# A one-core attention and MLP kernel: batch 0's Q by head halves, its first weights in row chunks, a tightened head chain, and batch 1's K^T V one step later

## The chip, the cores and the metric

The kernel runs on one core of one Trainium2 chip. The metric is the device time in microseconds (us) of one execution, as the median of several executions. Beside the time, each execution reports the **span**: the length from the core's first to its last instruction on the profile's clock. The time is a little longer than the span. I call the difference the **tail**. Each execution also reports the mean clock that the tensor engine was granted, 1.0 being full speed. Engines are called as the profile calls them: PE is the tensor engine's multiplies, PEld its weight loads, DVE the vector engine, ACT the scalar engine, POOL the GpSimd engine.

## The reference

```python
# q, k, v: (8 batches, 8 heads, 576 rows, 64), fp32
kv  = einsum('bhsd,bhse->bhde', k, v)            # 64 x 64 for each head
out = einsum('bhsd,bhde->bhse', q, kv)
rms = sqrt(mean(out * out, axis=-1) + 1e-6)
x   = (out / rms * g_norm)  # heads side by side: 4608 rows x 512
h   = x @ w_in              # 512 x 2048
g   = where(h > 0, h, exp(min(h, 0)) - 1)
return g @ w_out            # 2048 x 512
```

The kernel goes through nine groups of 512 rows: the first 512 of each of the eight batches, then the eight remainders of 64. Only the first group (batch 0) and the start of the second (batch 1) concern us. "Chunk c" is one of the four blocks of 128 columns of x, two heads each. "Half u" is two chunks.

## The kernel before

Loads are issued in this order: Q of batch 0, then K and V by chunk, then w_in by columns.

```python
    fetch_q(0)
    ...
    for c in range(4):
        fetch_packed_kv("k", 0, slice(c, c + 1))
        ...
        fetch_packed_kv("v", 0, slice(c, c + 1))
    edges = (0, 512, 768, 1280, 1664, 2048)
    for lo, hi in zip(edges, edges[1:]):
        load_w_in(slice(lo, hi))
    load_w_out(0, 4)
    fetch_packed_q(1)
    ...
```

The head of the kernel works on batch 0 chunk by chunk. Each chunk takes K^T V with its cast, the "scores" `se` (K^T V applied to Q), a square, a mean over 64 rows by a matmul, a logarithm, an exponential (together the reciprocal root), and a scale into `x0`. Idle matmuls on zeros stand between; they compute nothing and are meant to keep the tensor engine busy. Then come 24 products of x with the first 768 columns of w_in.

```python
    # ... chunks 0 to 2 alike, idle(...) between
    exp_first(1)
    idle(idle_ps, 1)
    kv_first(3)
    scale_first(0)
    idle(idle_ps, 1)
    mean0[2] = bank(2)
    mean_first(2)
    log_first(2)
    se0[3] = bank(3)
    se_first(3)
    square_first(3)
    exp_first(2)
    idle(bank(0), 2)
    scale_first(1)
    scale_first(2)
    # ... first(fs, cs): products of column blocks fs with chunks cs
    first((0, 1, 2, 3), (0,))
    mean0[3] = bank(2)
    mean_first(3)
    log_first(3); exp_first(3); scale_first(3)      # (one line each in the kernel)
    first((0, 1, 2, 3), (1, 2))
    first((4,), (0, 1, 2))
    first((0, 1, 2, 3), (3,))
    first((5,), (0, 1, 2))
    first((4, 5), (3,))
```

Batch 1's attention is woven into batch 0's second matrix product, `mm2` (output matmuls):

```python
    for j in range(J):                  # J = 4
        mm2_quarter(0, j, 1)
        if j == 1:
            at["kvu0"]()                # K^T V of half 0
        if j == 2:
            at["seu0"](scores)          # its scores, squares, sums
            at["sq0"]()
            at["sum0"]()
    for j in range(J):
        mm2(0, j, 8, 10)
        if j == 1:
            at["kvu1"]()
            at["inv0"]()
            at["mulu0"]()               # the two scales of half 0, on DVE
    ...
    for j in range(J):
        mm2(0, j, 10, 12)
        if j == 1:
            at["inv1"]()
            at["xu0"](scores[:, 0, :])  # eight transposes of half 0
```

## Time and profile before

| | before |
|---|---|
| time, median (range) | 284.17 us (284.08 to 284.18) |
| the execution with the profile | 284.47 us, span 282.7 |
| head ends (first of the next 24 matmuls, L465) | 20.43 us |
| batch 1's MLP starts | 46.85 us |
| PE busy | 98% of the span |

PE is busy nearly all the time, so a gain must come from removing work or from starting useful work sooner. The lines themselves are in the prediction.

### The profile page before, as it was taken

Reading aid. Unit: us, or ns where it says so; the run is one execution under the profiler, and the core shown is the slowest. Engines: PE = TensorE matmul, PEld = TensorE weight load, DVE = VectorE, ACT = ScalarE, POOL = GpSimd, SP = SyncE. Lnnn points to the kernel's source line nnn. Section 1 sums busy time; section 2 is a strip of 40 time slices with the busy share of each in tenths; the row PEclk is TensorE's granted clock in tenths of the full one; section 3 lists DMA queues with packets and bytes.
Section 4 is the critical chain, followed back from the end, with each engine's and each line's share of the span. In section 5 each row is a group of like instructions: output and inputs, shape, how many; then the busy total and the mean of one; then the engine's idle time right before and its main releaser. Section 6 shows DMA issues by size and latency. Waiting matters only on the chain.

```text
span 282.7 us, 5187 instructions
## 1 busy us (share of the span) xinstructions
PE 277.2 (98%) x2146; PEld 129.7 (46%) x2146; DVE 159.3 (56%) x231; ACT 154.5 (55%) x222; POOL 54.7 (19%) x96
## 2 busy tenths in 40 slices
PE   7999999999999999999999999999999999999994
PEld 3444454445444444444444444444444444444443
DVE  2359443878388646944694468445854585444400
ACT  2779546667487438533863377237923792333311
POOL 7834422261421331005200421012000000000000
PEclk9999999999999999999999999999999999999999
DMA  7999999797993696358935794455233122010122
GB/s 194 203 204 202 208 200 185 220 152 129 187 190 62 154 166 148 74 148 124 196 75 145 93 216 84 116 115 150 55 97 73 78 53 95 0 77 0 74 74 77
DMA packets 56523, 35.99 MB, mean 127 GB/s; under 512 B 32820, under 2 KB 54068, under 8 KB 56500
## 3 DMA queue, kind: packets, MB, share of 16 engines
q0 software_dynamic: 20752, 17.30, 39.9%
q1 hardware_dynamic: 35348, 17.83, 23.7%
q10 hardware_dynamic: 400, 0.52, 0.6%
q8 instruction: 17, 0.28, 0.4%
q14 instruction: 6, 0.05, 0.0%
HBM read 36.70 MB, written 9.44 MB: 163 GB/s over the span
## 4 chain that ended last, share of the span: by engine, by line
PE 95%; DMA 2%; DVE 1%; SPq 0%; issue 0%; ACT 0%
PE h_ps L465 41%; PE o_ps L512 39%; PE o_ps L917 5%; DMA st_q<-in_q_dram 2%; PE at L174 2%; PE bank L674 1%; PE at L465 1%; PE at L201 1%; PE h_ps L674 1%; PE bank L596 1%; PE bank L644 1%; PE se_ps L201 1%; PE kv_ps L174 0%; PE at L185 0%; PE se_ps L413 0%; PE bank L656 0%
## 5 line engine op out<-in xcount | busy, mean ns | idle before, releaser
L465 PE MATMUL h_ps<-xT,w_in_sb 128*128 128x512 bf16 x536 | 125.7, 379 | 0.0
L512 PE MATMUL o_ps<-w_out_sb,gT 128*128 128x512 bf16 x512 | 120.5, 379 | 0.0
L477 ACT ACTIVATE elu_e<-h_ps 128x1024 bf16<-128x1024 f32 (+1 forms) x71 | 70.0, 995 | 79.9 <-PE h_ps L465 78.3
L465 PEld LDWEIGHTS <-w_in_sb 128*128 128x128 bf16 x552 | 52.5, 98 | 63.2 <-DVE xT L333 1.7
L512 PEld LDWEIGHTS <-gT 128*128 128x128 bf16 x512 | 49.4, 98 | 58.4
L488 DVE TENSOR_SCALAR elu_e<-elu_e 128x1024 bf16<-128x1024 bf16 (+1 forms) x75 | 32.3, 431 | 72.9 <-ACT elu_e L477 72.9
L496 DVE TENSOR_TENSOR gT<-elu_e,h_ps 128x1024 bf16<-128x1024 bf16 (+1 forms) x51 | 60.1, 1179 | 5.7 <-DVE elu_e L488 0.5
L525 ACT COPY o_sb<-o_ps 128x512 f32<-128x512 f32 x32 | 18.6, 586 | 15.6 <-PE o_ps L512 15.6
L218 DVE TENSOR_REDUCE ss<-sq 128x16 f32<-128x1024 bf16 x16 | 19.4, 1219 | 10.8 <-ACT sq L213 10.1
L483 ACT ACTIVATE elu_h<-h_ps 128x1024 bf16<-128x1024 f32 (+1 forms) x20 | 19.5, 990 | 0.0
L150 POOL COPY q_bf<-q_pk 128x512 bf16<-128x512 bf16 x24 | 14.6, 638 | 21.6 <-DMA q_pk<-in_q_dram 21.6
L496 DVE TENSOR_TENSOR gT<-elu_e,elu_h 128x1024 bf16<-128x1024 bf16 x20 | 13.8, 692 | 2.9 <-ACT elu_h L483 1.5
L917 PE MATMUL o_ps<-w_out_sb,gT 128*128 128x512 bf16 (+1 forms) x80 | 14.1, 337 | 0.0
L125 POOL COPY gate<-qT 1x1 bf16<-1x1 bf16 x6 | 1.1, 182 | 63.7 <-DMA qT<-q_bf 63.7
L104 POOL DMA_DIRECT2D q_pk<-in_q_dram x14 | 10.6, 762 | 2.8 <-issue 1.1
L229 DVE TENSOR_TENSOR xs<-at,ss 128x512 bf16<-128x512 f32 x16 | 10.3, 682 | 1.2 <-ACT ss L225 1.2
L917 PEld LDWEIGHTS <-gT 128*128 128x128 bf16 x80 | 7.7, 98 | 6.4 <-DVE gT L496 0.4
L213 ACT ACTIVATE sq<-at 128x1024 bf16<-128x1024 f32 x9 | 9.4, 1043 | 1.6 <-PE at L201 1.0
L118 POOL DMA_DIRECT2D k_pk<-in_k_dram x12 | 8.3, 691 | 4.5 <-DMA w_in_sb<-in_moe_w_in_dram 2.9
L596 PE MATMUL bank<-zeros 128*128 128x512 bf16 x20 | 7.8, 515 | 1.2 <-DVE zeros L573 1.2
L118 POOL DMA_DIRECT2D v_pk<-in_v_dram x12 | 8.2, 684 | 3.7 <-DMA w_out_sb<-in_moe_w_out_dram 1.8
L925 ACT COPY o_last<-o_ps 128x512 f32<-128x512 f32 (+1 forms) x5 | 2.5, 501 | 10.8 <-PE o_ps L917 10.8
(79 smaller groups left out, 139.4 us busy)
## 6 DMA issues: line engine op xcount, KB each, us to landing
out_dram<-o_sb SPq DMA_DIRECT2D x16, 512.0 KB, 3.0
q_pk<-in_q_dram POOLq DMA_DIRECT2D x14, 256.0 KB, 4.8
k_pk<-in_k_dram POOLq DMA_DIRECT2D x6, 576.0 KB, 8.3
v_pk<-in_v_dram POOLq DMA_DIRECT2D x6, 576.0 KB, 10.8
st_q<-in_q_dram SPq DMA_DIRECT2D x2, 512.0 KB, 5.1
w_in_sb<-in_moe_w_in_dram POOLq DMA_DIRECT2D x2, 512.0 KB, 8.8
w_out_sb<-in_moe_w_out_dram POOLq DMA_DIRECT2D x2, 512.0 KB, 15.2
w_out_sb<-in_moe_w_out_dram POOLq DMA_DIRECT2D x4, 256.0 KB, 11.8
```

What stands on the lines that cost most here:

```text
L118: nc.gpsimd.dma_start(out=raw[name, b].rearrange("p h j d -> p h (j d)")[:, hs], in_=in_[:, hs])
L150: eng.tensor_copy(out=out_, in_=in_)
L218: nc.vector.reduce_sum(out=ss, in_=sq.rearrange("p c (h e) -> p (c h) e", h=H), axis=AX.X)
L465: nc.tensor.matmul(h_ps[a][:, cs], lhsT=w_in_sb[:, c, f * P : f * P + P], rhs=x(c, cs), start=(c == 0), stop=(c == KC - 1),)
L477: nc.scalar.activation(e[:, lo:hi, :], ps, AF.Exp)
L483: nc.scalar.activation(h[:, lo:hi, :], ps, AF.Relu)
L488: nc.vector.tensor_scalar(out=e[:, lo:hi, :], in0=e[:, lo:hi, :], scalar1=1.0, scalar2=1.0, op0=ALU.min, op1=ALU.subtract,)
L496: nc.vector.tensor_tensor(out=gT[T][:, 2 * i + lo : 2 * i + hi, :], in0=e[:, lo:hi, :], in1=h, op=ALU.add if relu else ALU.max,)
L512: nc.tensor.matmul(o_ps[T, j], lhsT=gT[T][:, f, j * P : j * P + P], rhs=w_out_sb[:, f, :], start=(f == 0), stop=(f == FC - 1),)
L525: nc.scalar.copy(o_sb[T][:, j % 2, :], o_ps.pop((T, j)))
L596: nc.tensor.matmul(ps, lhsT=zeros[:, 0:P], rhs=zeros, start=True, stop=True)
L917: nc.tensor.matmul(ps, lhsT=gT[B][:, f, j * P : j * P + P], rhs=w_out_sb[:, f, cols], start=(f == 0), stop=(f == FC - 1),)
```

## The change

The intent is to start the useful stream sooner. Q of batch 0 comes in two transfers of four heads each, so that chunk 0's pairs come first. The first 512 columns of w_in come in four row chunks, so that products of chunk 0 need only 128 KB. In the head, idle matmuls go and means and scales go up in the engines' order. Products run chunk by chunk. As batch 0 then ends sooner, batch 1's K^T V and scores move back by two to four output matmuls, so as not to wait for its inputs, and the first products of its MLP also run chunk by chunk (`by_c`, not in the cut below).

```diff
-    fetch_q(0)
-    q_raw0 = raw.pop(("q", 0))
+    q_raw0 = stage_tile("q")[:, 0:2048].rearrange("p (u x) -> p u x", u=2)
+    for u in range(2):
+        nc.sync.dma_start(...)          # heads 4u to 4u + 3
...
-    edges = (0, 512, 768, 1280, 1664, 2048)
+    for c in range(KC):
+        load_w_in(slice(0, 512), slice(c, c + 1))
+        if c == 1:
+            load_w_in(slice(512, 768))
+    edges = (768, 1024, 1280, 1664, 2048)
...
+    g_ps = bank(2)                      # the g column, from further down
     kv_first(0)
-    idle(idle_ps, 1)
+    turn_last(7, 1)
...
     kv_first(2)
-    idle(idle_ps, 2)
+    mean0[1] = bank(0)
+    mean_first(1)
+    log_first(1)
...
     exp_first(1)
+    scale_first(0)
     idle(idle_ps, 1)
     kv_first(3)
-    scale_first(0)
-    idle(idle_ps, 1)
...
-    idle(bank(0), 2)
...
-    first((0, 1, 2, 3), (1, 2))
-    first((4,), (0, 1, 2))
-    first((0, 1, 2, 3), (3,))
-    first((5,), (0, 1, 2))
-    first((4, 5), (3,))
+    first((0, 1, 2, 3), (1,))
+    first((4,), (0, 1))
+    first((0, 1, 2, 3, 4), (2, 3))
+    first((5,), range(KC))
...
         mm2_quarter(0, j, 1)
-        if j == 1:
+        if j == 2:
             at["kvu0"]()
-        if j == 2:
-            at["seu0"](scores)
-            at["sq0"]()
-            at["sum0"]()
+    at["seu0"](scores)
+    at["sq0"]()
+    at["sum0"]()
     for j in range(J):
         mm2(0, j, 8, 10)
-        if j == 1:
+        if j == 2:
             at["kvu1"]()
...
-        if j == 0:
+        if j == 2:
             at["xu1"](scores[:, 1, :])
```

More of the change, by code (lines that the diff above doesn't have):

```diff
@@ L133, in unpack_q, with load_w_in @@
             copy_on(eng, bf["q", b][:, j], t[:, :, j])
-    def load_w_in(cols):
+    def load_w_in(cols, cs=slice(0, KC)):
         nc.gpsimd.dma_start(
-            out=w_in_sb[:, :, cols], in_=moe_w_in.rearrange("(c p) f -> p c f", p=P)[:, :, cols]
+            out=w_in_sb[:, cs, cols],
+            in_=moe_w_in.rearrange("(c p) f -> p c f", p=P)[:, cs, cols],
         )
@@ L444, with mm1 @@
     gT = {}
-    def mm1(T, i, cols=(slice(0, 512),), relu=False, home="m1", between=()):
+    def mm1(T, i, cols=(slice(0, 512),), relu=False, home="m1", between=(), by_c=False):
         if i == 0:
@@ L461, in mm1 @@
         for cs in cols:
-            for a in range(2):
+            steps = [(a, c) for a in range(2) for c in range(KC)]
+            if by_c:
+                steps.sort(key=lambda step: step[1])
+            for a, c in steps:
                 f = 2 * i + a
-                for c in range(KC):
-                    nc.tensor.matmul(
-                        h_ps[a][:, cs],
-                        lhsT=w_in_sb[:, c, f * P : f * P + P],
-                        rhs=x(c, cs),
-                        start=(c == 0),
-                        stop=(c == KC - 1),
-                    )
+                nc.tensor.matmul(
+                    h_ps[a][:, cs],
+                    lhsT=w_in_sb[:, c, f * P : f * P + P],
+                    rhs=x(c, cs),
+                    start=(c == 0),
+                    stop=(c == KC - 1),
+                )
         return elu(T, i, parts, relu, between)
@@ L549 @@
     V, A, Q = nc.vector, nc.scalar, nc.gpsimd
-    fetch_q(0)
-    q_raw0 = raw.pop(("q", 0))
+    q_raw0 = stage_tile("q")[:, 0:2048].rearrange("p (u x) -> p u x", u=2)
+    for u in range(2):
+        nc.sync.dma_start(
+            out=q_raw0[:, u].rearrange("p (h x) -> p h x", h=4),
+            in_=q[0, 4 * u : 4 * u + 4, 0:G, :].rearrange("h (p j) d -> p h (j d)", j=J),
+        )
     packed_kv(0)
@@ L603 @@
     idle(idle_ps, 9)
-    q_st = q_raw0.rearrange("p (q h j d) -> p q j h d", q=4, h=2, j=J)
+    q_st = q_raw0.rearrange("p u (l s j d) -> p u s j l d", l=2, s=2, j=J)
     q_two = attp.tile([P, NPAIR, J, 2, D], BF16, name="q_two", tag="q_two", bufs=1)
@@ L608, in cast_first @@
     def cast_first(pair, eng):
-        copy_on(eng, q_two[:, pair], q_st[:, pair])
+        copy_on(eng, q_two[:, pair], q_st[:, pair % 2, pair // 2])
     def turn_first(ps, pairs):
@@ L619 @@
     cast_first(0, V)
-    cast_first(1, A)
+    cast_first(2, A)
     qt_ps = turned(3)
-    turn_first(qt_ps, (0, 1))
-    nc.vector.tensor_copy(out=qT0[:, 0:2], in_=qt_ps)
+    turn_first(qt_ps, (0, 2))
+    nc.vector.tensor_copy(
+        out=qT0.rearrange("p (s u) t -> p u s t", u=2)[:, 0], in_=qt_ps
+    )
     idle(idle_ps, 4)
-    cast_first(2, V)
+    cast_first(1, V)
     cast_first(3, A)
@@ L680, in first, with turn_last @@
                 )
-    qt_ps = turned(7)
-    turn_first(qt_ps, (2,))
-    nc.scalar.copy(qT0[:, 2, :], qt_ps[:, 0, :])
+    def turn_last(n, pair):
+        qt_ps = turned(n)
+        turn_first(qt_ps, (pair,))
+        nc.vector.tensor_copy(out=qT0[:, pair, :], in_=qt_ps[:, 0, :])
+    g_ps = bank(2)
+    nc.tensor.matmul(
+        g_ps[:, 0:1],
+        lhsT=g_row.rearrange("p l d -> p (l d)"),
+        rhs=one,
+        start=True,
+        stop=True,
+    )
+    nc.vector.tensor_copy(out=g_col, in_=g_ps[:, 0:1])
     kv_first(0)
-    idle(idle_ps, 1)
+    turn_last(7, 1)
     se0[0] = bank(6)
@@ L689 @@
     square_first(0)
-    qt_ps = turned(0)
-    turn_first(qt_ps, (3,))
-    nc.vector.tensor_copy(out=qT0[:, 3, :], in_=qt_ps[:, 0, :])
-    idle_ps = bank(3)
+    turn_last(0, 3)
     kv_first(1)
@@ L701 @@
     exp_first(0)
-    g_ps = bank(1)
-    nc.tensor.matmul(
-        g_ps[:, 0:1],
-        lhsT=g_row.rearrange("p l d -> p (l d)"),
-        rhs=one,
-        start=True,
-        stop=True,
-    )
-    nc.vector.tensor_copy(out=g_col, in_=g_ps[:, 0:1])
     kv_first(2)
-    idle(idle_ps, 2)
+    mean0[1] = bank(0)
+    mean_first(1)
+    log_first(1)
+    idle_ps = bank(3)
     se0[2] = bank(1)
@@ L715 @@
     square_first(2)
-    mean0[1] = bank(0)
-    mean_first(1)
-    log_first(1)
     exp_first(1)
+    scale_first(0)
     idle(idle_ps, 1)
     kv_first(3)
-    scale_first(0)
-    idle(idle_ps, 1)
     mean0[2] = bank(2)
@@ L734 @@
     pair = ps_head.tile([P, 2, G], FP32, name="h_ps", tag="kv")
-    products = {0: pair[:, 0, :], 1: pair[:, 1, :], 2: bank(6), 3: bank(7), 4: bank(0)}
+    products = {0: pair[:, 0, :], 1: pair[:, 1, :], 2: bank(6), 3: bank(0), 4: bank(7)}
     first((0, 1, 2, 3), (0,))
@@ L873 @@
     for i in range(8):
-        mm1(1, i, relu=i in (1, 4), home={0: "at", 2: "m2", 5: "m2"}.get(i, "m1"))()
+        mm1(1, i, relu=i in (1, 4), home={0: "at", 2: "m2", 5: "m2"}.get(i, "m1"), by_c=i == 0)()
         if i == 3:
```

## The prediction

> **What bounds the kernel now.** I began with the page's busy shares, then cut the span into stretches, then followed the chain that ended last through the first 50 us, and last read single instructions there in order of time. First the shares, then three of the stretches (length, then busy time and count of PE, PEld, DVE, ACT and POOL, granted clock, DMA share, GB/s).
>
> ```profile
> PE 277.2 (98%) x2146; PEld 129.7 (46%) x2146; DVE 159.3 (56%) x231; ACT 154.5 (55%) x222; POOL 54.7 (19%) x96
> ```
>
> ```profile
> 8.00:14.87 6.87, 6.73 (x101) 3.14 (x99) 2.78 (x8) 5.15 (x9) 5.33 (x8) 1.00 1.25 203
> 14.87:20.43 5.56, 5.56 (x26) 2.44 (x26) 2.28 (x4) 3.90 (x8) 2.15 (x3) 1.00 1.29 205
> 28.69:46.85 18.16, 18.16 (x219) 9.14 (x218) 8.97 (x12) 9.57 (x15) 5.99 (x9) 1.00 1.26 205
> ```
>
> The tensor engine has work at nearly all times, so only what it does that is not needed, or waits that its busy time hides, can be won. From 14.87 us on its stream is useful: the chain steps 1.73 us for 8 matmuls without a break. Before that it is filled with idle matmuls on zeros, so "busy" means nothing there. The question is when the useful stream starts. The chain (start, length, what):
>
> ```profile
> 14.00 0.33 PE bank L644 x2
> 14.33 0.54 PE bank L596 x2
> 14.87 0.50 PE h_ps L674 x2
> 15.37 0.43 PE bank L674 x2
> ...
> 18.49 0.43 PE h_ps L674 x2
> 18.92 1.51 PE bank L674 x7
> 20.43 5.18 PE h_ps L465 x24
> ```
>
> L596 is idle work right ahead of the first product. The 24 products of the head (L674) and one mean matmul take 14.87 to 20.43, 5.56 us, of which 25 x 0.216 = 5.4 are floor. So the product block has no hole worth filling; only its start can move. What holds the start, from the view in order of time (start, length, engine, what, idle before):
>
> ```profile
> 12.56 0.60 ACT L653 ACTIVATE sq<-bank 128x512 bf16<-128x512 f32 x1 [0.37 <-PE bank L644]
> 13.06 0.68 ACT L659 ACTIVATE r<-bank,eps_col 128x512 f32<-128x512 f32 x1
> 13.50 0.29 DVE L638 CAST kv<-kv_ps 64x128 bf16<-64x128 f32 x1 [1.52 <-PE kv_ps L174]
> 13.77 0.63 ACT L662 ACTIVATE r<-r 128x512 f32<-128x512 f32 x1
> 13.83 1.41 DVE L665 SCALAR_TENSOR_TENSOR xT<-bank,g_col,r 128x512 bf16<-128x512 f32 x2
> 14.76 0.55 PEld L674 LDWEIGHTS <-w_in_sb 128*128 128x128 bf16 x4 [0.39 <-DMA w_in_sb<-in_moe_w_in_dram]
> ```
>
> Two gates close together. The first weights wait for one 512-column transfer that lands at 14.68 (issued 7.38, 7.3 to landing). The first scale of x comes only at 13.83, although its exponential ended at 12.19: it stands behind the last K^T V cast in the vector engine's order.
>
> **What the Trainium skill says.** (1) "TensorE: Matmul & The Clock Gate", Back-to-back issue gap: N/2.4 + 2.5 ns, 216 ns at N = 512. The trace agrees: 1.73 us for 8. (2) Same page, Part 1 on the clock gate: the array runs at half rate after about 3.4 us of idleness. The trace has the two states: the first nine idle matmuls start 0.43 us apart, products 0.216. (3) "ScalarE: Activation LUTs", What ACT_TABLE_LOAD costs: an activation takes about 186 ns + 0.833 N, a pointer bias adds 93, and neighbours overlap by 93; N = 512 gives 613 and 706. The trace has 594 for the square, 685 for the logarithm. (4) "Perfetto Trace Analysis", DMA Optimizations: splitting a DMA may let some of the work start sooner where the engines are otherwise idle. Here they are not: 203 to 205 GB/s through all three stretches. So row chunks only change which bytes land first.
>
> **The change, part by part.**
>
> *Q by head halves.* The old halves gave pairs 0 and 1 first, but scores of chunk 0 need pairs 0 and 2, and pair 2 came with the half that landed at 7.26. The new first half (landing about 4.94) has 0 and 2. Chunk 0 then waits only for K^T V, whose V lands at 7.82 (1.92 + 5.9). Before, the chain is cast 7.30, transposes 7.79, K^T V 8.18, its cast 8.63, scores 8.96. After, the tiny g matmul (0.31) now sits at about 7.7, K^T V 8.0 to 8.4, cast to 8.75, the pair-1 transposes (0.40) beside that cast, scores about 8.8. Gain 0.15 us. The ACT copy of 0.59 leaves the scalar engine, where nothing much stood behind it.
>
> *Tightened chain.* ACT does 4 squares, 4 logarithms, 4 exponentials. Start to start back to back they take 0.48, 0.57, 0.54 (11.08 to 11.56, 14.31 to 14.88, 13.77 to 14.31), 1.59 a chunk. V chunks land at about 7.82, 9.28, 10.69, 12.16, one per 1.46 us, and K^T V cannot go before them. Playing the new order through with the old durations: square 0 at 9.30, logarithm 0 at 10.39 (mean 0 now after the second K^T V), square 1 10.96, exponential 0 11.44, logarithm 1 12.02 (13.06 before, since its mean now precedes scores 2), square 2 12.59, exponential 1 13.07, logarithm 2 13.67, square 3 14.24, exponential 2 14.72, logarithm 3 15.30 (16.05), exponential 3 16.02 to 16.65 (17.40). Scale 0, now ahead of the last cast, 12.12 to 12.83; scale 1 to 14.46; scale 2 to 16.15; scale 3 to 17.40 (18.18 before).
>
> *Row chunks of w_in.* The bytes ahead of products 0 to 5 are the same, so the last of them lands as the old second transfer did, at 8.1 + 8.9 = 17.0. In between, 128 KB chunks at some 0.65 us (an estimate: the 512 KB landed 2.52 after the last V): chunk 0 about 12.8, chunk 1 13.4, columns 512 to 768 about 15.1, chunk 2 15.8, chunk 3 16.5 to 17.0.
>
> *Products.* The last scores end about 13.8; nothing idle stands behind them. Four products of chunk 0: 13.9 to 14.7. Mean 3 waits for square 3 (14.83): 14.9 to 15.1, a hole of some 0.2. Then 4 + 2 + 5 = 11 products, 2.4 us, to 17.48; chunk 3 of x is ready at 17.4, so no hole. Then 5 + 4 = 9 products, 1.94: end 19.42. Before 20.43. The two limits (order on PE, last scale) meet within 0.1, so I take **1.0 us** for the head.
>
> *Batch 1.* The PE's work is the same; places differ. K^T V of half 0 moves from behind 24 to behind 28 output matmuls, scores 0 from 28 to 32, K^T V 1 from 36 to 38; the transposes of half 0 stay behind 44, those of half 1 go from 58 to 62. The moves are needed: V of half 1 lands at 25.92 + 11.9 = 37.8 and K^T V 1 starts at 38.92 before; one microsecond earlier it would touch. But the first half's chain now has four matmuls (0.86 us) less:
>
> ```profile
> 38.18 1.22 DVE L218 TENSOR_REDUCE ss<-sq 128x16 f32<-128x1024 bf16 x1 [6.08 <-ACT sq L213]
> 39.55 0.31 ACT L224 ACTIVATE ss<-ss,eps_col 128x16 f32<-128x16 f32 x1
> 39.89 0.22 ACT L225 ACTIVATE ss<-ss 128x16 f32<-128x16 f32 x1
> 40.14 1.29 DVE L391 TENSOR_TENSOR xs<-se_ps,ss 128x512 bf16<-128x512 f32 x2 [0.74 <-ACT ss L225]
> 41.48 0.61 PE L413 MATMUL se_ps<-ident,xs 128*128 128x128 bf16 x8
> ```
>
> On the old clock: reduce 38.18 + 0.86 = 39.04 to 40.26; logarithm 40.30; exponential to 40.86; scale 40.89 to 42.18. The PE reaches its transposes at 41.60; the first four need only the first scale (41.55), done at 41.85; the others wait until 42.22. A hole of **0.37 us** that was not there (the scale ended at 41.43, 0.17 before). Half 1's transposes have room: scale 1 ends near 45.35, they stand at 46.0. Its x is then late for the first MLP matmuls, which is what chunk-first order there is for: 2 + 4 matmuls, 1.3 us, over a vector pass of 0.75. No cost.
>
> *Behind that* the chain is PE alone to the end, every piece at its 1.73 or 1.83, and I see no absolute time that a shift would touch: V of batch 2 lands at 50.1, its K^T V starts at 53.76. So the shift should reach the end whole: 1.0 - 0.37 = 0.63. **284.17 - 0.63 = 283.55 us.**
>
> **Rivals.** *A. The landing of the weights takes over.* Chunk 3 of w_in near 17.0 against a need at 17.48 leaves 0.5 us, columns 512 to 768 about 0.8; smaller transfers may lag more. For it: the old 256 KB transfer landed 2.3 us behind the one ahead of it, as long as 512 KB took. Then the head gives 0.3 to 0.6 and the total is 283.9 to 284.2. *B. No hole in batch 1* (K^T V and scores come earlier against ACT and DVE than I think): 283.2. *C. Batch 1's inputs land later*, since there are four more transfers to issue and each issue waits for an old landing (POOL waits on w_in landings for 1.24 to 1.67 us at a time): the wait is moved, not removed, total near 284.2 or above. Against: by K of half 1 the order of waits is the old one again, and the queue never empties. *D. The clock gate closes*, for of the seven idle matmuls after the first thirteen only one is left: PE is then about 78% busy from 8 to 14 us (4.6 of 5.9 us). Products at half rate would cost 2 us or more: 285.5 to 287. Against: no hole is longer than 0.5 us.
>
> **Range and chances.** Head 0.5 to 1.2, hole 0 to 0.5, repeats of the kernel within 0.1: low 282.9 (1.2 and no hole), high 284.2 (A or C). D has a chance of some 4%. Two per cent is 5.7 us, more than the whole idle work of the head, so within 2% is all but sure.
>
> **What would show it.** First product near 13.9 (14.87), exponential 3 ending near 16.65 (17.40), first L465 counterpart near 19.4 in the chain (20.43): the head is right. No tensor wait on w_in: A is wrong. A gap of 0.3 to 0.4 us within the first eight transposes of batch 1, released by the vector scale: the hole is right. Matmul spacing of 0.43 in the head: D. I am wrong if the start of batch 1's MLP (46.85) does not move by 0.6, or if it does and the end does not.

## The result and the profile after

| | before | after |
|---|---|---|
| time, median (range) | 284.17 us (284.08 to 284.18) | 285.16 us (284.73 to 285.50) |
| ratio of the kernels, 95% interval | | 1.0035, 1.0017 to 1.0052 |
| spans of four timed executions | | 282.9, 283.1, 282.8, 283.2 |
| tails of the same four | | 2.6, 1.95, 1.93, 2.07 |

A ratio is the mean time of one kernel's fast runs over that of the other's of the same rounds, so it is not quite the ratio of the medians. The time rose by 1.0 us where I had predicted a fall of 0.6, and 285.16 lies outside my range of 282.9 to 284.2. Two kernels below have executions at a lower clock; they are named.

First the page of the changed kernel, its busy shares (x counts instructions):

```profile
PE 275.4 (97%) x2140; PEld 129.1 (46%) x2140; DVE 160.7 (57%) x232; ACT 153.7 (54%) x221; POOL 57.1 (20%) x100
```

Six matmuls fewer than before (2140 against 2146), the idle ones. PE is busy for 1.8 us less. That time was not won, so there must be new holes. The stretches of the head (length, then busy time and count by engine, clock, DMA share, GB/s) show where:

```profile
8.00:13.90 5.90, 5.26 (x93) 2.62 (x87) 3.12 (x8) 4.33 (x8) 5.19 (x8) 1.00 1.22 187
13.90:19.50 5.60, 5.08 (x24) 2.10 (x23) 1.88 (x3) 3.41 (x6) 3.81 (x6) 1.00 1.37 199
```

Before, the product stretch was busy 5.56 of 5.56 us. Now 0.52 of 5.60 is empty. And the queue moved 187 GB/s ahead of it, where before it moved 203. The chain that ended last (start, length, what) says for what PE waited:

```profile
9.56 7.25 DMA w_in_sb<-in_moe_w_in_dram
...
16.86 0.60 PE h_ps L687 x2
17.47 0.65 PE bank L687 x3
...
20.06 5.18 PE h_ps L468 x24
```

The chain now runs through a transfer of w_in, from 9.56 to 16.82 us. Before, it ran through PE alone here. The head ends at 20.06, and 20.43 before: 0.37 of the predicted 1.0 us. The view in order of time has the single instructions:

```profile
13.67 0.61 PE L687 MATMUL h_ps<-xT,w_in_sb 128*128 128x512 bf16 x2
...
15.80 0.63 ACT L675 ACTIVATE r<-r 128x512 f32<-128x512 f32 x1
...
16.46 0.75 DVE L678 SCALAR_TENSOR_TENSOR xT<-bank,g_col,r 128x512 bf16<-128x512 f32 x1 [0.55 <-ACT r L675]
...
16.86 0.60 PE L687 MATMUL h_ps<-xT,w_in_sb 128*128 128x512 bf16 x2 [0.53 <-DMA w_in_sb<-in_moe_w_in_dram]
```

The first product starts at 13.67 and the last exponential ends at 16.43 (15.80 + 0.63), both a little earlier than predicted. The hole is at the first product of chunk 2, and the weights end it.

How the weights of chunk 2 came to land at 16.82 is seen part by part. A transfer signals its sixteen parts one by one. The Trainium skill, "DMA: Bandwidth & Descriptors", section "Why a DMA increments its semaphore by 16 and not by 1", says that the engines finish independently and that only the full 16 means that all has landed. The trace agrees. These are the moments of the semaphore's first, fifteenth and sixteenth steps in the changed kernel's trace, worked out from the semaphore records:

```
transfer of w_in       first   15th    16th
rows 0, cols 0-512     12.38   12.84   13.01
rows 1, cols 0-512     13.04   13.54   13.73
cols 512-768           14.44   14.84   15.04
rows 2, cols 0-512     15.09   15.64   16.82
rows 3, cols 0-512     15.74   16.30   17.02
cols 768-1024          17.07   17.69   18.19
cols 1024-1280         18.42   19.01   19.48
```

Fifteen parts of chunk 2 were there at 15.64, earlier than my 15.8. The sixteenth came 1.18 us later, and one part stays 0.5 to 0.7 us behind in the transfers after it. It looks as if one of the sixteen engines had been held up for about a microsecond. The view of the DMA queues for 14.5 to 17.2 us (packets, MB, share of the sixteen engines) has just one packet that is not the kernel's own:

```profile
q8 instruction: 1, 0.02, 2.2%
```

It is a 16 KB transfer of the queue named "instruction", from 14.78 on, 0.948 us long. In all fourteen traces such a transfer comes at 14.40 to 15.27 us, and the sixteenth part of the w_in transfer then under way, or of the next, comes 0.55 to 1.52 us after the fifteenth. In the trace of the kernel before (taken again) the second w_in transfer had fifteen parts at 15.88 and the last at 16.90. There it cost nothing, since its weights were first used at about 17.2. The trace doesn't name the engine that moved a packet, and no experiment took the instruction transfer away. So that it makes the part late is argued from time and repetition, not shown. Nor is every lag of this kind: in the first trace of the kernel before, the sixteenth part came 0.34 to 0.51 us after the fifteenth in every K, V and w_in transfer from 6.41 us on, ahead of any such packet.

Now batch 1. The chain of the changed kernel, then that of the kernel before:

```profile
40.51 1.30 DVE xs L392 x2
...
41.85 0.61 PE se_ps L414 x8
42.46 3.88 PE o_ps L515 x18
...
47.22 1.73 PE at L468 x8
```

```profile
41.60 0.49 PE se_ps L413 x8
42.09 3.02 PE o_ps L512 x14
...
46.85 1.73 PE at L465 x8
```

The 0.37 us that the head was ahead is now 0.37 behind (42.46 against 42.09, 47.22 against 46.85). So this passage cost 0.74 us. The view in order of time shows its first two instructions:

```profile
41.26 0.10 PEld L414 LDWEIGHTS <-xs 128*128 128x128 bf16 x1 [0.52 <-DVE xs L392]
...
41.85 0.61 PE L414 MATMUL se_ps<-ident,xs 128*128 128x128 bf16 x8 [0.62 <-DVE xs L392]
```

The weight load of the first transpose went at 41.26, when the first scale was done. Its matmul waited until the second scale was done as well, at 41.81. In the built program this matmul has a wait of its own on DVE. Its target lies in the tile of the scores, which the second scale still reads; that this is the reason is inferred.

Third, the tails. The profiled execution took 285.5 us for a span of 282.9. Its trace has a last instruction transfer of 16 KB at 284.62, 1.118 us long, after the last instruction. In the two traces of the kernel before, the last of these transfers lies at 275.7 and 275.3, inside the span. Of the fourteen traced executions one more, that of after_rows_first below, had a tail above 1.95 (2.07), and it too has a last transfer behind its last instruction, at 285.05 and 1.36 long. In both the transfer ends 0.24 us after the measured time (285.74 against 285.5, 286.41 against 286.17). In the other twelve it ends before that time, also in after_batch1_old, where it starts behind the last instruction (282.99 to 284.08, time 284.21) and the tail is normal. So the traces fit an execution that can't end before this transfer. Two cases are no proof, and which engine's instructions it carries is open.

### The profile page after: what moved, and what is told of

The parts are those of the page before. It is cut to its first block, busy times and chain, and to the rows that moved or that the text cites. A ratio compares the mean times of both kernels' runs of the same rounds, so it can differ in the third digit from the quotient of the medians.

```text
span 282.9 us, 5177 instructions
## 1 busy us (share of the span) xinstructions
PE 275.4 (97%) x2140; PEld 129.1 (46%) x2140; DVE 160.7 (57%) x232; ACT 153.7 (54%) x221; POOL 57.1 (20%) x100
## 4 chain that ended last, share of the span: by engine, by line
PE 91%; DMA 5%; DVE 1%; ACT 1%; POOL 1%; issue 1%; POOLq 0%
PE h_ps L468 41%; PE o_ps L515 38%; PE o_ps L925 5%; DMA w_in_sb<-in_moe_w_in_dram 3%; DMA k_pk<-in_k_dram 2%; PE at L175 2%; PE at L468 1%; PE at L202 1%; PE bank L687 1%; POOL w_in_sb L136 1%; PE se_ps L202 1%; DVE xs L392 0%; DVE ss L219 0%; PE se_ps L414 0%; PE h_ps L687 0%
## 5 line engine op out<-in xcount | busy, mean ns | idle before, releaser
L499 DVE TENSOR_TENSOR gT<-elu_e,elu_h 128x1024 bf16<-128x1024 bf16 x20 | 14.5, 727 | 2.2 <-ACT elu_h L486 0.8
L175 PEld LDWEIGHTS <-k_pk 64*64 64x64 bf16 x576 | 6.4, 107 | 4.9 <-issue 4.6
```

The source lines that it names most:

```text
L175: nc.tensor.matmul(kv_ps[l * 64 : l * 64 + 64, s, u * 64 : u * 64 + 64], lhsT=bf["k", T][rows, j, 2 * u + l, :], rhs=bf["v", T][rows, j, 2 ...
L499: nc.vector.tensor_tensor(out=gT[T][:, 2 * i + lo : 2 * i + hi, :], in0=e[:, lo:hi, :], in1=h, op=ALU.add if relu else ALU.max,)
```

## The experiments

My theory had three parts: the head gains less since chunk 2's weights come late; batch 1's hole is bigger than predicted; and the rest is in the tail and goes with the number of PE instructions. Against them stood that the tail is chance, that all of the loss is in batch 1, and that the row chunks themselves are what costs. Each expectation quoted below says in its own words which of them it sets against which. Kernels of one set ran on one chip and share its runs of the kernel before.

**Set 1, chip 14; before: 284.0 us, span 282.2.**

*after_again*: the changed kernel unaltered, five rounds.

> The changed kernel itself, unaltered. Its time (285.16) is 0.99 us above before, but its span from first to last instruction (282.9) only 0.2 above, so 0.8 us lies outside the span. Theory 1: in the first trace a 16 KB transfer of the instruction queue (1.12 us long) comes at 284.62, after the last instruction; in before the last such transfer is at 275.70, hidden. If so, it comes back in this run at the same place, and the time is again 284.7 to 285.5. Theory 2: another chip or a throttled clock (0.998 in that run): then on one chip with before the difference shrinks to the span's, 0.2 to 0.4 us.

Measured: 284.67 us (283.9 to 285.6), ratio 1.0026 (1.0011 to 1.0041). The spans' median is 282.75, half a microsecond above before. Five tails are 1.76 to 1.81, one is 2.71. Neither theory fits whole: the traced execution had its last instruction transfer at 277.08, inside the span, and the difference is 0.67, not 0.2 to 0.4. The rise is real, and on this chip mostly in the span. The spans scatter from 282.1 to 283.8 where those of before lie at 282.2 to 282.3; what moves them is open. In its trace the instruction transfer came at 15.20 instead of 14.78: now chunk 2 was complete at 16.16, and chunk 3 had its fifteenth part at 16.81 and its last at 17.36. The late part moves with the instruction transfer. And chunk 2's weights, first used at 16.73 by this chain, no longer hold PE:

```profile
16.73 0.43 PE h_ps L687 x2
...
19.76 0.65 PE h_ps L468 x3
```

This is the earliest end of the head among the seven traces of the new head, though its first product started 0.39 later (14.06 against 13.67). From first product to head end it took 5.70 us, in the first trace 6.39. So the same kernel shows the head with the late landing and without it.

*after_six_more*: six small matmuls on zeros after the last product, nothing else, so that the count is 2146 again.

```diff
+    spare = ps_m2.tile([P, DM], FP32, name="spare", tag="mm2")
+    for _ in range(6):
+        nc.tensor.matmul(spare[:, 0:64], lhsT=zeros[:, 0:P], rhs=zeros[:, 0:64], start=True, stop=True)
```

> The changed kernel with six small matmuls on zeros behind the last product, so that the tensor engine has as many instructions (4291) as before, not 4279. Nothing waits for them. Theory 1: the instruction transfer moves back to about 276 us and the time falls by 0.6 to 0.9 us against the changed kernel, to 284.2 to 284.6, with the span unchanged at 282.9. Theory 2: six matmuls at the end change nothing (285.2 or a little more).

Measured: 284.86 us (284.48 to 284.95), ratio 1.0027 (1.0015 to 1.0039). It did not get faster than after_again, since its spans were longer (283.1). But all its tails were 1.75 to 1.90. So the tail behaves as expected and the time does not: on this chip the tail isn't the main loss.

*before_six_less*: the kernel before without six of its late idle matmuls (its count is that of the changed kernel).

```diff
     kv_first(0)
-    idle(idle_ps, 1)
...
     kv_first(2)
-    idle(idle_ps, 2)
...
     scale_first(0)
-    idle(idle_ps, 1)
...
-    idle(bank(0), 2)
+    bank(0)
```

> The kernel before without six of its seven late idle matmuls of the head: 4279 tensor instructions, as the changed kernel has; the first product still waits for the w_in landing at 14.68. Theory 1: span within 0.2 of before (282.7), yet the time rises by 0.6 to 0.9 us, to about 284.9, with an instruction transfer after the end. Theory 2 (idle matmuls are off the path): time 284.2. If the clock gate needed these idles, products would stand 0.43 us apart and the span would grow by 2 us.

Measured: 284.02 us, ratio 1.003 (0.9998 to 1.0063). Four executions took 283.96 to 284.02, exactly the time of before. All six tails were normal (1.76 to 1.92), so **the theory that the count alone makes the tail fell.** The other two executions took 286.59 and 286.68 at a granted clock of 0.988 and 0.987. PE's busy time in this kernel's head:

```profile
8.00:14.30 6.30, 4.72 (x85) 2.41 (x79) 2.68 (x8) 4.89 (x9) 5.00 (x7) 1.00 1.24 203
```

PE is busy for 75% here (4.72 of 6.30; in the changed kernel 5.26 of 5.90, 89%). So the idle matmuls win nothing in the usual run, but seem to be an insurance: a third of the executions without them lost 2.6 us at a lower clock. The slow two were not traced.

*after_batch1_old*: the changed kernel with batch 1's places of before.

```diff
-        if j == 2:
+        if j == 1:
             at["kvu0"]()
-    at["seu0"](scores)
-    at["sq0"]()
-    at["sum0"]()
+        if j == 2:
+            at["seu0"](scores)
+            at["sq0"]()
+            at["sum0"]()
...                                # kvu1 back to j == 1, xu1 back to j == 0
```

> The changed kernel with K^T V, scores and transposes of batch 1 where before has them; its head is kept. In the trace of the changed kernel the tensor engine waits 0.62 us before the first transposes of batch 1 and the batch costs 0.74 us in the chain (0.37 ahead at 20.06, 0.37 behind at 47.22). Theory: the wait vanishes, span and time fall by 0.7 us against the changed kernel (about 282.2 and 284.4). Rival: without the moves K^T V of half 1 meets the landing of its V (37.8) and waits as long: no gain.

Measured: 284.75 us (284.21 to 285.17), ratio 1.0032 (1.0019 to 1.0045), with three of five tails long (2.09, 2.65, 2.77). The spans' median is 282.4, so 0.35 better than after_again. The chain now goes through a landing:

```profile
26.32 12.26 DMA v_pk<-in_v_dram
...
38.72 0.48 PE at L175 x36
```

V of half 1 lands at 38.58 and K^T V starts right after it. So the moves are indeed needed for a head this early, but without them batch 1 costs only some 0.34 us in its trace: from the head's end (19.97) to the transposes (41.48) it takes 21.51 us, and 21.17 in the kernel before (20.43 to 41.60). They avoid a wait and bring a larger one. The theory (wait gone, 0.7 us) and its rival (no gain) each got half.

**Set 2, chip 3; before: 284.23 us, span 282.4.**

*before_again*: the kernel before, for a second trace.

> The kernel before, unaltered, for a second trace of it. Its first trace (span 282.7, time 284.47) was 0.3 us slower than its timed runs (284.0 to 284.2, spans 282.2). Theory: the first 512 columns of w_in usually land about 14.2 and not at 14.68, so products start near 14.3 and the head ends near 19.95, not 20.43; then the head of the changed kernel (20.06, 19.76, 20.11, 19.97 in four traces) gains nothing on it. Rival: the head ends at 20.4 here too and the 0.3 to 0.5 us lie elsewhere.

Measured: 284.19 us, span 282.4, ratio 0.9999. The head's end in its chain:

```profile
20.12 5.18 PE h_ps L465 x24
```

That is 0.31 earlier than in the trace from which I predicted, and between the theory (19.95) and its rival (20.4). Three traces with the head of before give 20.43, 20.12 and 20.25 (mean 20.27). The seven with the new head and 512-column row chunks give 19.76 to 20.19 (mean 20.02). The head's gain is 0.25 us by these means, which is no more than the spread within each group (0.31 and 0.43). The old order without six idle matmuls (before_six_less), whose first weights landed at 14.26, even ends its head at 19.96. So the gain is not sure.

*before_batch1_new*: the kernel before with batch 1's part of the change alone.

```diff
-        if j == 1:
+        if j == 2:
             at["kvu0"]()
...                                # as the last part of the change, and by_c for the first product of batch 1
```

> The kernel before with only the batch 1 part of the change (K^T V, scores and transposes later, chunk-first order in the first products of batch 1). Theory: the wait before the first transposes of batch 1 appears here too and costs 0.75 us in span and time: 283.0 and 284.75, each time the same within 0.2, since the tensor instructions (4291) are as before. Rival: the wait is there only because the new head runs ahead: no change (284.0).

Measured: 285.00 us (284.88 to 285.06), span 283.2, ratio 1.0026 (1.0013 to 1.0039), all tails normal. This part alone costs 0.77 us (285.00 - 284.23), as much as the whole change did on chip 14. Its chain:

```profile
40.70 1.30 DVE xs L391 x2
...
42.04 0.61 PE se_ps L413 x8
```

The eight transposes again go only after both scales (40.70 + 1.30 = 42.00).

*after_turn_late*: the changed kernel, with the eight transposes of half 0 behind 48 output matmuls in place of 44.

```diff
             at["inv1"]()
+        if j == 3:
             at["xu0"](scores[:, 0, :])
```

> The changed kernel with one thing moved: the transposes of half 0 of batch 1 stand behind 48 output matmuls, not 44, so behind 0.86 us more work. Theory: the wait of 0.62 us before them vanishes and nothing takes its place; against the changed kernel span and time fall by 0.7 us, to spans of 281.6 to 282.2. Rival: the scalar pass behind these transposes comes too late for the first products of batch 1 and the wait moves there: less than 0.3 us gained.

Measured: 284.58 us (283.76 to 285.92), ratio 1.0015 (0.9996 to 1.0035), span 282.3. Three of six tails were 2.72 to 2.79. Its chain:

```profile
42.10 0.45 PE se_ps L414 x8
...
46.44 1.73 PE at L468 x8
```

Batch 1's MLP starts 0.78 us earlier than in the changed kernel (46.44 against 47.22), with the head at the same 20.06. The hole is gone, and it was as large as the part cost by itself. The long tails hide the gain: the fastest execution is 283.76, below all of before's here.

*after_rows_first*: all four row chunks ahead of columns 512 to 768.

```diff
     for c in range(KC):
         load_w_in(slice(0, 512), slice(c, c + 1))
-        if c == 1:
-            load_w_in(slice(512, 768))
+    load_w_in(slice(512, 768))
```

> The changed kernel with row chunks 2 and 3 of w_in ahead of columns 512 to 768 in the queue; products in the same order. In the changed kernel chunk 2 landed at 16.82 though 15 of its 16 parts were there by 15.64: a 16 KB instruction transfer (0.95 us, at 14.78) held one engine. Theory: then chunk 2 lands by about 14.6, chunk 3 by 15.3, and columns 512 to 768 take the blow, at 16.8 to 17.0; the wait is then at f = 4 of chunk 0 (wanted at 15.7) and is longer, 1.0 to 1.3 us: head ends at 20.4 to 20.8. Rival (row chunks are slow in themselves): chunk 2 still lands after 16.

Measured: 285.69 us (285.55 to 286.17), ratio 1.0056 (1.0044 to 1.0068), a clear loss.

```profile
17.64 0.61 PE bank L686 x2
...
21.27 5.18 PE h_ps L468 x24
```

Chunks 2 and 3 landed at 14.22 and 15.29, early enough, but columns 512 to 768 at 17.59, with fifteen parts at 16.77, and the products of column block 4 come before those of chunk 2. They were wanted at about 15.85 (PE waited 1.79 us, to 17.64), so fifteen parts alone would have been 0.9 late: half of the wait is the new order, half the late part (0.82). In these traces the late part strikes whichever transfer is under way. An order of transfers that suits the products doesn't escape it; the products would have to be reordered too.

**Set 3, chip 7; before: 284.29 us, span 282.4.** The long tails were gone with the six matmuls back (after_six_more), so I combined both cures and then varied the w_in transfers on that base.

*turn_late_six*: after_turn_late with the six matmuls of after_six_more.

> The changed kernel with the transposes of half 0 four output matmuls later (no wait in batch 1) and with six small matmuls behind the last product, so 4291 tensor instructions as before. In the runs so far, time less span was 1.73 to 1.93 in all 31 executions of kernels with 4291, but 2.6 to 2.8 in seven of 27 of the changed kernel's kin with 4279. Theory: all tails 1.7 to 1.9; spans 281.9 to 282.6 as with the transposes late alone; so time 283.7 to 284.4, median about 284.0, 0.2 below before. Rival: tails of 2.7 come here too.

Measured: 283.74 us (283.49 to 284.02), ratio 0.9978 (0.9967 to 0.9990), span 282.0, tails 1.74 to 1.82. **It beats both kernels**, by 0.55 us over before and by more over the changed one.

*wide_turn_six*: the same, with the first 768 columns in four row chunks.

```diff
     for c in range(KC):
-        load_w_in(slice(0, 512), slice(c, c + 1))
-        if c == 1:
-            load_w_in(slice(512, 768))
+        load_w_in(slice(0, 768), slice(c, c + 1))
```

> As turn_late_six, but w_in's first 768 columns in four row chunks, so no transfer of columns 512 to 768 stands ahead of chunk 2. Estimate from the landings seen: chunk 2 (15 parts) at 15.3, its last part by 16.4 with the instruction transfer in the way, wanted at 16.3; chunk 3 about 17.0, wanted at 17.3. Theory (the late last part of chunk 2 is the head's loss): the hole of 0.5 us shrinks under 0.15, head ends at 19.5 to 19.7, time 0.4 us below turn_late_six, about 283.6. Rival (splitting itself slows the queue): chunk 2 or 3 lands as late as now and nothing is gained.

Measured: 283.63 us (283.5 to 284.1), ratio 0.9977 (0.9965 to 0.9988). That is 0.1 below turn_late_six, no difference that these runs resolve. Its chain:

```profile
16.67 0.60 PE h_ps L685 x2
...
19.87 5.18 PE h_ps L468 x24
```

Chunk 2 landed at 16.63, with fifteen parts at 15.11. The theory failed: the hole is as before.

*whole_turn_six*: the same, with w_in's columns 0 to 512 and 512 to 768 as two whole transfers, as before the change.

```diff
-    for c in range(KC):
-        load_w_in(slice(0, 512), slice(c, c + 1))
-        if c == 1:
-            load_w_in(slice(512, 768))
-    edges = (768, 1024, 1280, 1664, 2048)
+    edges = (0, 512, 768, 1280, 1664, 2048)
```

> As turn_late_six, but w_in's first columns in whole transfers of 512 and 256 columns, as before. Theory: the first product waits for the 512 columns (14.3 to 14.7) and then runs without a hole, since x is ready earlier than before: head ends at 19.8 to 20.2, as with row chunks (20.0 on average): the chunks bring nothing, time equal within 0.2. Rival: row chunks bring 0.4 us or more.

Measured: 284.42 us, ratio 1.0016 (0.9994 to 1.0039). Two of six executions had a clock of 0.994 and took 285.72 and 285.80; the other four average 284.25, still 0.5 above turn_late_six. Its chain:

```profile
15.00 0.61 PE h_ps L683 x2
...
20.62 5.18 PE h_ps L468 x24
```

The landing at 14.96 holds the first product and the head ends at 20.62, 0.43 later than in turn_late_six (20.19). So the row chunks are worth some 0.4 us here in spite of the late part. The times say so too, but the trace alone would be weak: in the four other traces with a whole first transfer it landed at 14.26 to 14.72. That the chunks are the loss is refuted.

**Set 4, chip 0; before: 284.13 us, span 282.3.**

*turn_late_six_early*: turn_late_six with its six matmuls ahead of the first K^T V in place of behind the last product.

```diff
     nc.vector.tensor_copy(out=g_col, in_=g_ps[:, 0:1])
+    for _ in range(6):
+        nc.tensor.matmul(idle_ps[:, 0:64], lhsT=zeros[:, 0:P], rhs=zeros[:, 0:64], start=True, stop=True)
     kv_first(0)
```

> As turn_late_six, with the six small matmuls in the head, where the tensor engine waits for V of batch 0 anyway (6.9 to 7.8 us), and not behind the last product. Theory (the number of tensor instructions ahead of the end decides where the last 16 KB instruction transfer falls): tails of 1.7 to 1.9 in all executions, a last instruction transfer at 275 to 278, span 281.8 to 282.3, time about 283.8. Rival (the six matmuls at the end help by being the last work, not by their number): tails of 2.0 to 2.8 in some executions, as without them.

Measured: 284.35 us (283.97 to 284.59), ratio 1.0009 (0.9995 to 1.0022), span 282.5, all tails 1.76 to 1.91. With the six matmuls in the head no long tail came either, so it isn't their place at the end. But the time is no better than before's. This was on another chip than turn_late_six, and the six stand in the head. Which of these matters is open. The gain of turn_late_six rests on one set.

**The tails, counted.** Over the experiments, the kernels with 2146 matmuls have 75 executions, with tails of 1.73 to 1.95 all. The changed kernel and its kin with 2140 have 26, of which 11 are above 1.95 and seven between 2.6 and 2.8. (Some of the expectations quote this count as it stood or was miscounted then.) before_six_less has 2140 too and six normal tails. So with six PE instructions more the changed kernel showed no long tail, but the count is not the whole rule.

## Why the prediction was wrong

The sum predicted was -1.0 + 0.37 = -0.63 us. What the runs showed is -0.25 (head), +0.77 (batch 1) and, in the first set, +0.34 (tail: mean 2.14 against the usual 1.8). That makes +0.86 of the +0.99 measured. The rest of 0.13 is not accounted for. On chip 14, the same with a tail of +0.14 makes +0.66, against 0.67 measured. That it meets so well is partly luck: the terms come from other chips and single traces, and the head's term is no larger than its spread.

**Q by halves and the tightened chain: right.** First product predicted 13.9, was 13.67. Exponential 3 ending at 16.65, was 16.43. Last scale ending at 17.40, was 17.21.

**"11 products, 2.4 us, to 17.48; chunk 3 of x is ready at 17.4, so no hole": this step failed.** I held two limits side by side, the order on PE and the last scale, and allowed only a margin on the third, the landing of w_in. The estimate for the last chunk, 17.0, was right (17.02). The one for chunk 2, 15.8, was right for fifteen parts (15.64) and wrong for the sixteenth (16.82). The hole is 0.59 us (PE's last product before it ended at 16.27, the next started at 16.86). PE had been 0.13 ahead of my count there (15.1 and six products make 16.40), and the first pair behind the hole took 0.60 in place of 0.43: together 0.63 of the 0.64 between 19.42 predicted and 20.06. In after_again's trace the weights were in time, and the hole is absent. It is rival A, at a transfer I had not named: I gave the margins of chunk 3 and of columns 512 to 768.

**The base was one trace.** The head of before ended at 20.43 in it, at 20.12 and 20.25 in two others. So of the 0.37 us between the first two traces only 0.25 remain on average. In the base trace the first 512 columns had fifteen parts at 14.21 and the last at 14.72; in the second trace, at 14.41 and 14.48. The gate that I wanted to remove was partly a late sixteenth part of that one execution.

**The hole in batch 1: foreseen, but twice as large.** The scale ended at 41.81 (predicted 42.18) and PE was ready at 41.22 (predicted 41.60): both moments are near 0.37 early, so the chain was right. The step that failed is "the first four need only the first scale": the first transpose's matmul waited for the second too, so none could go. The term of 0.37 was a wait of 0.62, and the eight transposes behind it took 0.61 in place of 0.49: together 0.74, and 0.77 by itself in before_batch1_new. The experiments confirm it from both sides, by adding the part alone and by moving only the transposes. Rival B is refuted. Whether transposes into another tile would let four of them go after the first scale was not tried.

**"The moves are needed": right, for the wrong balance.** after_batch1_old waits for V, some 0.34 us. Rival C is right in part: V of half 1 landed at 38.58 there, at 38.24 in the changed kernel, and at 37.8 before. The moves were sized against that wait, but the transposes of half 0 were not moved with them. That is the one line of after_turn_late.

**"The shift should reach the end whole": right for the span as far as seen, incomplete for the time.** The medians of the spans on chip 14 rose by 0.55, and head and batch 1 make 0.52. I had treated the time as the span plus a constant. The tail is no constant for this kernel.

**Rival D** did not happen in the changed kernel: its clocks were 0.997 to 1.0, and PE was 89% busy ahead of the products, not 78%. A lower clock appeared in before_six_less and in whole_turn_six, in two of six executions each. Whether it is what D describes is not shown, as none of the four was traced.

## What to carry to other kernels

When a piece that starts a chain on other engines is moved back, move what ends the chain as well, and check in the built program which instruction carries the wait: here the first of eight transposes waited for a scale that only the later ones needed. A landing is as late as its slowest sixteenth, so leave a microsecond where a small transfer gates the tensor engine at a moment when foreign packets were seen (in these traces the last part lagged by up to 1.52 us there). Look at span and tail apart, and at more than one trace of the base, before a term of some tenths of a microsecond is believed.

## What the Trainium skill lacked or had wrong

- "Trainium Architecture — The Big Picture", section "The software stack", says that the instruction streams are moved to the engines when the program is loaded. The traces show 16 or 17 transfers of 16 KB on a queue named "instruction" all through the execution, 0.88 to 2.07 us long each, and in three of the fourteen traces one behind the last instruction (in the changed kernel at 284.62 us). Other pages of the skill do tell of such refills while a program runs, so this page alone is at odds with the traces.
- "DMA: Bandwidth & Descriptors", section "Why a DMA increments its semaphore by 16 and not by 1": independent engines are there, as seen. How far one may lag is not: fifteen parts at 15.64 us, the sixteenth at 16.82, and 0.5 to 0.7 us in each of the transfers behind it.
- "Perfetto Trace Analysis", section "DMA Optimizations" says that splitting may bring the whole task to an earlier end where DMA engines are generally idle. Here they moved 193 to 202 GB/s in both traces of the pair, and row chunks still brought 0.43 us (head end 20.19 against 20.62), since what counts is the order in which bytes land. In the changed kernel's stretch ahead of the products the rate was lower than before, 187 against 203 GB/s.
- "TensorE: Matmul & The Clock Gate", Part 1, names idleness of about 3.4 us as what halves the clock. before_six_less had PE 75% busy in its head, and two of its six executions had a mean clock of 0.987 and 0.988 and took 2.6 us more. They were not traced, so where the clock was low is open.
- No page that I found says that the tail can change from one kernel or execution to the next: 1.73 to 1.95 us in 75 executions of kernels with 2146 matmuls, up to 2.8 in the changed kernel and its kin with 2140, and normal again with six small matmuls more.
